# Half of w1 in row blocks of 128, 128, 96 and 96: a decode step with cached attention and a small dense layer

## The chip, the cores and the metric

The kernel runs on one core of one Trainium2 chip. The metric is the device time of one execution in microseconds (us); the median of several runs is compared. Differences of about 0.2% of this kernel's time can be told from no change.

## The reference

The kernel mixes two branches by a gate that is computed from the input:

```python
x = A_x                                            # [2, 1, 448]
g = sigmoid((x * gate_w).sum(-1, keepdims=True))
q = (x @ wq) as 16 heads of 256
p = softmax(q . k_cache * 256**-0.5)               # over 4096 cached keys
a = (p . v_cache, heads joined) @ wo               # [2, 1, 448]
b = relu(x @ w1) @ w2                              # w1 [448, 1792], w2 [1792, 448]
return g * a + (1 - g) * b
```

Everything is float32. The caches are [2, 16, 4096, 256] each; with the weights some 290 MB are read for one output of 2 x 448 numbers.

## The kernel before

The work of attention is cut into U = 32 units, one for each pair of batch and head. A unit's keys and values lie in DRAM as one row of 65,536 B for each of 128 partitions, 8.4 MB. On the chip there is a ring of three slots of that size (SLOTS, `slot`). SP issues all loads, in the order in which they are written in `sync` (L153 on): at first the query weights `wq` into slot 0 together with the input's columns `xg`, then kv 0 and 1 (L67 to L69, before the block); kv 2 when the query matmuls are done (L156); then, in a loop, the next unit into a slot as soon as DVE has freed it (L161, L162). Two loads stand in the queue at any time. The tail of the list is written out: the last kv unit in two halves (L167, L168), `w1` and `w2` into slot 0 (L170, L171) once unit 30 is freed from it, and `wo` in six pieces into slot 1 (L175), last the output (L178).

For a unit PE computes the scores from the keys (L131), DVE their maximum (L351), ACT the exponential and its sum (L318), and DVE eight products with the values (L356), the last of which signals `freed`.

The dense layer and the joining lie in `pe_tail`. `hidden` computes x @ w1 in the PSUM tile `pa`. The 1792 columns of w1 are four groups g of FG = 448; group g fills partitions 32g to 32g+31 of `pa`, each row holding x of one of the two batch entries, repeated. The 448 rows of w1, over which is contracted, are three blocks c of 128 (`x_of(c)`, L111) and a last one of 64. The blocks of 64 of two column groups are stacked on 128 partitions and contracted in one matmul of 64 output rows with `xl`, a tile that has x in one half and zeros in the other (L114). So `hidden` has 3 x 4 + 2 = 14 matmuls; each appears twice in the trace, as two passes for float32. It is called in three parts, between which PE does the small steps of the softmax tail: blocks 0 and 1 after the wait for `w1_in` (L231, L232); then, after the last unit is freed, two transposes (L234, L235) and block 2; then, after `wb_ok`, one small matmul and the last block. ACT applies the relu (L327), PE transposes (L250, L252), ACT copies (L329, L332), and PE accumulates the product with w2 in `acc` (L258). The wo product is accumulated in the same tile (L270) as its pieces land; DVE copies `acc` (L375), and PE folds it into `z` with the last pieces of wo (L278, L283), which DVE copies for the output (L377).

At the start ACT makes the broadcast copies of x: `xr` for the blocks of 128, `xn` for the gate, `xl` for the stacked blocks of 64 (L297 to L301); the last of them signals `x_ok`, for which PE's first matmul waits (L193).

Of the kernel before, what the change touches and what calls it, by code (L numbers as in the profile page):

```python
# [4 lines left out]
AF = mybir.ActivationFunctionType  # L5
# [4 lines left out]
P, HP = 128, 64  # L10
G = 4
R = P // G
# [3 lines left out]
DIRECT = (3, 2, 1)  # L16


def gated_mix_decode(nc, wq, kv, wm, wo, out):
    U, _, SW = kv.shape  # L20
    D = 448
    B = 2
    RB = R // B
# [4 lines left out]
    KC, KF = 4, 3  # L28
    H = U // B
    HH = H // G  # L30
    NW = wq.shape[1] - KC * (B + 1)
    FG = 448
    NF = 14
    W1 = 2 * (2 * KF * FG + FG)
    DG = D // G
    NO = HH * J
    SCALE = float(DH) ** -0.5
    pe, dve, act, pool, sp = nc.tensor, nc.vector, nc.scalar, nc.gpsimd, nc.sync
# [12 lines left out]
    slot = [ring[:, i * SW:(i + 1) * SW] for i in range(SLOTS)]  # L51

    def sb(name, *shape):
        t = nc.alloc_sbuf_tensor(name, list(shape), F32)
        assert nc.sbuf_base <= first
        return t.ap()
# [6 lines left out]
    last_v, w1_in, w2_in = ev(), ev(), ev()  # L63
# [11 lines left out]
    xr = sb("xr", P, KF, P // B, B)  # L75
    xl = sb("xl", P, 2, RB, B)
    xn = sb("xn", P, P // B, B)
    ge = sb("ge", P, 1)
    gp = sb("gp", P, 1)
    omg = sb("omg", P, 1)  # L80
# [7 lines left out]
    p = sb("p", P, SG)  # L88
# [10 lines left out]
    pa = ps("pa", P, CW)  # L99
# [5 lines left out]
    def x_of(c, n=R):  # L105
        return xr[:, c].rearrange("p r b -> p (r b)")[:, :n]

    def project(dst, w, at, at_last, n, lo, hi):
        for c in range(lo, min(hi, KF)):
            for g in range(G):  # L110
                m = pe.matmul(dst[g * R:(g + 1) * R, :n], x_of(c), w[:, at(c, g):at(c, g) + n], start=(c == 0), stop=False)  # L111
        if hi == KC:
            for i in range(2):
                m = pe.matmul(dst[i * HP:(i + 1) * HP, :n], xl.rearrange("p j r b -> p (j r b)"),  # L114
                              w[:, at_last(i):at_last(i) + n], start=False, stop=True)
        return m

    xg = slot[0][:, NW:wq.shape[1]].rearrange("p (c b) -> p c b", c=KC)

    ident_0, ident_ok, par_ok, fold_ok, xl_0 = (ev() for _ in range(5))  # L120
    x_ok, gate_mm, gate_ok, ge_ok, gp_ok, omg_ok = (ev() for _ in range(6))
# [23 lines left out]
    ml_tr, nb_ok, e_ok, el_ok, rl_ok, wb_ok, wp_mm, os_ok, po_mm, oc_ok = (ev() for _ in range(10))  # L145
    acc_mm, a_ok, z_mm, res_ok = ev(), ev(), ev(), ev()
    w1 = slot[0][:, :W1]
    w2 = slot[0][:, W1:W1 + NF * D]
    w_o = slot[1]

    with nc.Block(no_gpsimd_drain=True) as block:

        @block.sync  # L153
        def _(_e):
            sp.wait_ge(q_mm, 2)
            sp.dma_start(slot[0], kv[2]).then_inc(slot_in[0], 16)  # L156
            with nc.Fori(0, LOOP - 2, engines=(ET.SP,)) as r:
                u0 = sp.snap(r * SLOTS)
                for k in range(SLOTS):
                    s = (k + 1) % SLOTS  # L160
                    sp.wait_ge(freed, u0 + k + 1)  # L161
                    sp.dma_start(slot[s], kv[bass.ds(u0 + k + SLOTS, 1)].rearrange("o p n -> (o p) n")  # L162
                                 ).then_inc(slot_in[s], 16)
            sp.wait_ge(freed, U - 4)
            sp.dma_start(slot[1], kv[U - 2]).then_inc(slot_in[1], 16)
            sp.wait_ge(freed, U - 3)
            sp.dma_start(slot[2][:, :SW // 2], kv[U - 1][:, :SW // 2]).then_inc(slot_in[2], 16)  # L167
            sp.dma_start(slot[2][:, SW // 2:], kv[U - 1][:, SW // 2:]).then_inc(last_v, 16)  # L168
            sp.wait_ge(freed, U - 2)
            sp.dma_start(w1, wm[:, :W1]).then_inc(w1_in, 16)  # L170
            sp.dma_start(w2, wm[:, W1:]).then_inc(w2_in, 16)  # L171
            sp.wait_ge(freed, U - 1)
            k = 0
            for n, s in zip(ACC + DIRECT, wo_in):
                sp.dma_start(w_o[:, k * D:(k + n) * D], wo[:, k * D:(k + n) * D]).then_inc(s, 16)  # L175
                k += n
            sp.wait_ge(res_ok, 1)
            sp.dma_start(out, res[0:7 * 15 + 1:7, :]).then_inc(out_sem, 16)  # L178
# [13 lines left out]
        def pe_main():  # L192
# [7 lines left out]
            for i in range(2):  # L200
                if i:
                    pe.wait_ge(q_ok, i)
                project(pb, slot[0][:, i * NW // 2:(i + 1) * NW // 2], lambda c, g: g * W + c * CW,
                        lambda i: G * W + i * CW, CW, 0, KC).then_inc(q_mm, 1)
# [18 lines left out]
                pe.end_ifs()  # L223

        def pe_tail():
            half = W1 // 2
            def hidden(lo, hi):
                return project(pa, w1, lambda c, g: g // 2 * half + (g % 2 * KF + c) * FG,
                               lambda i: i * half + 2 * KF * FG, FG, lo, hi)

            pe.wait_ge(w1_in, 16)  # L231
            hidden(0, 2)  # L232
            pe.wait_ge(freed, U)
            pe.transpose(pc[:U, :P], nm, ident)  # L234
            pe.transpose(pc[:U, P:2 * P], ls, ident).then_inc(ml_tr, 1)  # L235
            hidden(2, KF)
            pe.wait_ge(wb_ok, 1)
            pe.matmul(pb[:, :U], wb.rearrange("u g r -> u (g r)"), ident[:U, :U], start=True,
                      stop=True).then_inc(wp_mm, 1)
            hidden(KF, KC).then_inc(hid_mm, 1)  # L240
            pe.wait_ge(fold_ok, 1)
            pe.wait_ge(os_ok, 1)
            n = HH * B * J
            for g in range(G):
                m = pe.matmul(pc[g * R:(g + 1) * R, :n], sel,
                              os.rearrange("p u j -> p (u j)")[:, g * n:(g + 1) * n], start=True, stop=True)
            m.then_inc(po_mm, 1)
            pe.wait_ge(hid_ok, 1)
            for t in range(KF):
                pe.transpose(pb[:, t * P:(t + 1) * P], hs[:, t * P:(t + 1) * P], ident)  # L250
            for j in range(2):
                m = pe.matmul(pb[j * HP:(j + 1) * HP, KF * P:], hs[:, KF * P:], ident, start=True, stop=True)  # L252
            m.then_inc(hid_tr, 1)
            pe.wait_ge(w2_in, 16)
            pe.wait_ge(hr_ok, 1)
            for k in range(NF):
                g = k % G
                pe.matmul(acc[g * R:(g + 1) * R, :D], hr[:, k, :], w2[:, k * D:(k + 1) * D], start=(k < G),  # L258
                          stop=False)

            def o_of(k):
                return oc[:, k // J, k % J].rearrange("p r b -> p (r b)")

            pe.wait_ge(oc_ok, 1)
            k, n = 0, sum(ACC)
            for i, a in enumerate(ACC):
                pe.wait_ge(wo_in[i], 16)
                for _ in range(a):
                    g = k % G
                    m = pe.matmul(acc[g * R:(g + 1) * R, :D], o_of(k), w_o[:, k * D:(k + 1) * D], start=False,  # L270
                                  stop=(k >= n - G))
                    k += 1
            m.then_inc(acc_mm, 1)
            for i, a in enumerate(DIRECT):
                if i == 0:
                    pe.wait_ge(a_ok, 1)
                    for g in range(G):
                        pe.matmul(z[g * R:(g + 1) * R, :DG], fold.rearrange("p r b -> p (r b)"),  # L278
                                  a_sb[:, g * DG:(g + 1) * DG], start=(i == 0), stop=False)
                pe.wait_ge(wo_in[len(ACC) + i], 16)  # L280
                for _ in range(a):
                    for g in range(G):
                        m = pe.matmul(z[g * R:(g + 1) * R, :DG], o_of(k),  # L283
                                      w_o[:, k * D + g * DG:k * D + (g + 1) * DG], start=False,
                                      stop=(k == NO - 1))
                    k += 1
            m.then_inc(z_mm, 1)
# [7 lines left out]
        def _(_e):  # L295
            act.wait_ge(slot_in[0], 16)
            act.activation(xr, xg[:, :KF, None, :B].to_broadcast([P, KF, P // B, B]), AF.Copy)  # L297
            act.activation(xn, xg[:, KF:, :B].to_broadcast([P, P // B, B]), AF.Copy)
            act.wait_ge(xl_0, 1)
            for j in range(2):  # L300
                a = act.activation(xl[j * HP:(j + 1) * HP, j], xg[j * HP:(j + 1) * HP, KF:, :B]  # L301
                                   .to_broadcast([HP, RB, B]), AF.Copy)
            a.then_inc(x_ok, 1)
            act.wait_ge(gate_mm, 1)
# [1 line left out]
            for i in range(2):  # L306
# [3 lines left out]
                a = act.activation(qt[:, i * U // 2:(i + 1) * U // 2, :].rearrange("p (s n) t -> p s t n", s=2),  # L310
                                   pc.rearrange("p (s t x) -> p s t x", s=2, t=T)[:, :, :, ::17], AF.Copy)
# [18 lines left out]
            for j in range(2):  # L330
                r = slice(j * HP, (j + 1) * HP)
                a = act.activation(hr[r, KF * G:, :],  # L332
                                   pb[r, KF * P + j * HP:KF * P + (j + 1) * HP].rearrange("p (k r) -> p k r", r=R),
                                   AF.Copy)
# [103 lines left out]
```

## Time and profile before

| | |
|---|---|
| median of 3 runs | 676.48 us (676.44 to 677.43) |
| the profiled execution | 676.38 us |
| its span, first to last instruction | 674.8 us |
| mean granted TensorE clock | 0.676 |
| read from DRAM | 289.54 MB, 429 GB/s over the span |
| busy: PE, DVE, ACT | 213.0, 339.8, 54.2 us |
| DMA packets | 6082 |

The engines' busy times say how much of the span each one works. The profile's slices divide the span into 40 equal parts and give for each a tenth of busy share by engine, the clock, and what the DMA engines moved. The row of a DMA queue gives packets, megabytes and the time that the packets took, as a share of sixteen DMA engines' span. The chain that ended last is followed back from the last instruction; a row of it says when a piece began, how long it lasted and whose work it was. A row of the timeline gives the start, the duration, the engine and line, the operation, and in brackets the idle time before it with what ended it. A row of the view of windows gives, for one stretch, the length, each engine's busy time, the granted clock, the DMA share and the rate.

### The profile page before, as it was taken

What the parts mean: (1) busy time and instruction counts of PE and PEld (TensorE: products, weight loads), DVE (VectorE), ACT (ScalarE), POOL (GpSimd) and SP (SyncE); (2) the same over time, 40 slices, a digit from 0 to 9 for tenths busy, and PEclk for the clock granted to TensorE, in tenths of its full rate; (3) what the DMA queues carried; (4) which work ended last, traced back from release to release, by engine and by line L of the source; (5) the groups of instructions that cost most, each with busy time, mean ns of one, the idle gap of its engine ahead of it and who ended that gap; (6) DMA issues with size and microseconds to landing.
All of it is one profiled execution on the core that took longest, in us unless ns stands there. A gap on an engine that the chain in (4) does not pass through costs nothing.

```text
span 674.8 us, 4173 instructions
## 1 busy us (share of the span) xinstructions
PE 213.0 (32%) x1279; PEld 52.0 (8%) x1279; DVE 339.8 (50%) x561; ACT 54.2 (8%) x144; POOL 1.1 (0%) x9
## 2 busy tenths in 40 slices
PE   0633221333332123333321233333222333332455
PEld 0210000000000000000000000000000000000011
DVE  0024566545455665544656654455566445456670
ACT  0110000000000000000000000000000000000110
POOL 0000000000000000000000000000000000000000
PEclk9976567767655676776656677665667767655879
DMA  9999999999999999999999999999999999999997
GB/s 381 427 435 436 435 435 435 435 435 435 435 435 435 435 435 435 435 435 435 431 435 435 435 435 435 435 435 435 435 435 435 435 435 435 435 435 406 420 437 304
DMA packets 6082, 289.59 MB, mean 429 GB/s; under 512 B 704, under 2 KB 832, under 8 KB 1216
## 3 DMA queue, kind: packets, MB, share of 16 engines
q1 hardware_dynamic: 6080, 289.55, 99.3%
q8 instruction: 2, 0.03, 0.0%
HBM read 289.54 MB, written 0.01 MB: 429 GB/s over the span
## 4 chain that ended last, share of the span: by engine, by line
DMA 70%; DVE 12%; PE 9%; issue 6%; DVEq 1%; ACT 1%; SPq 0%; ACTq 0%
DMA ring<-in_kv 65%; DVE ring L356 10%; PE sc L131 9%; DMA ring<-in_wo 4%; DVE nm L351 2%; DVEq L356 1%; ACT p L318 1%; PE z L283 0%; DVEq L348 0%; DVEq L353 0%; PE acc L270 0%; SPq L175 0%; SPq L162 0%; DVEq L351 0%; DVE a_sb L375 0%
## 5 line engine op out<-in xcount | busy, mean ns | idle before, releaser
L356 DVE SCALAR_TENSOR_TENSOR ring<-ring,p 128x1024 f32 x256 | 295.9, 1222 | 54.8 <-ACT p L318 54.8
L131 PE MATMUL sc<-ring,qc 128*32 128x512 f32 x1024 | 182.6, 878 | 417.8 <-DMA ring<-in_kv 417.8
L351 DVE TENSOR_REDUCE nm<-sc 128x1024 f32 x32 | 39.2, 1225 | 236.1 <-PE sc L131 236.1
L131 PEld LDWEIGHTS sc<-ring,qc 128*32 128x32 f32 x1024 | 41.2, 154 | 558.6 <-issue 558.6
L318 ACT ACTIVATE p<-sc,nm 128x1024 f32<-128x1024 f32 x32 | 35.7, 1114 | 257.8 <-DVE nm L351 257.8
L323 ACT ACTIVATE ov<-on 128x8 f32 x32 | 6.7, 208 | 309.0 <-DVE ring L356 309.0
L356 DVE DVE_READ_ACCUMULATOR ring<-ring,p 128x1 f32 x256 | 21.4, 83 | 0.0
L343 DVE TENSOR_SCALAR ge<-ge 128x1 f32<-128x1 f32 x1 | 0.2, 155 | 21.5 <-ACT ge L305 21.5
L196 PE MATMUL pa<-ring,xr 128*128 128x1 f32 x6 | 1.4, 356 | 21.4 <-ACT xl L301 21.4
L375 DVE COPY a_sb<-acc 128x448 f32<-128x448 f32 x1 | 0.6, 625 | 14.7 <-PE acc L270 14.7
L111 PE MATMUL pa<-ring,xr 128*32 128x448 f32 x24 | 4.2, 830 | 11.7 <-DMA ring<-in_wm 11.7
L270 PE MATMUL acc<-ring,oc 128*32 128x448 f32 x52 | 5.9, 544 | 4.7 <-DMA ring<-in_wo 4.7
L111 PE MATMUL pb<-ring,xr 128*32 128x512 f32 x48 | 7.1, 737 | 0.0
L318 ACT ACTIVATION_READ_ACCUMULATOR p<-sc,nm x32 | 6.2, 193 | 0.0
L320 ACT ACTIVATE qc<-qt x32 | 6.1, 192 | 0.0
L258 PE MATMUL acc<-ring,hr 128*32 128x448 f32 x28 | 3.2, 541 | 1.0 <-ACT hr L332 1.0
L196 PEld LDWEIGHTS pa<-ring,xr 128*128 128x128 f32 x6 | 1.4, 326 | 21.4 <-ACT xl L301 21.4
L270 PEld LDWEIGHTS acc<-ring,oc 128*32 128x32 f32 x52 | 1.7, 109 | 8.9 <-issue 5.9
L114 PE MATMUL pb<-ring,xl 128*64 128x512 f32 x8 | 2.2, 618 | 0.0
L297 ACT ACTIVATE xr<-ring 128x384 f32<-128x384 f32 x1 | 0.5, 522 | 18.3 <-DMA ring<-in_wq 18.3
L111 PEld LDWEIGHTS pb<-ring,xr 128*32 128x32 f32 x48 | 1.6, 132 | 3.9 <-issue 3.9
L308 ACT ACTIVATE q<-pb 128x512 f32<-128x512 f32 x2 | 1.2, 598 | 8.6 <-PE pb L114 8.6
(56 smaller groups left out, 23.7 us busy)
## 6 DMA issues: line engine op xcount, KB each, us to landing
ring<-in_kv SPq DMA_DIRECT2D x2, 4096.0 KB, 34.7
ring<-in_wq SPq DMA_DIRECT2D x1, 7174.0 KB, 19.5
ring<-in_wm SPq DMA_DIRECT2D x2, 3136.0 KB, 30.7
ring<-in_wo SPq DMA_DIRECT2D x1, 3136.0 KB, 24.4
ring<-in_wo SPq DMA_DIRECT2D x1, 1792.0 KB, 28.3
ring<-in_wo SPq DMA_DIRECT2D x1, 896.0 KB, 30.0
ring<-in_wo SPq DMA_DIRECT2D x1, 672.0 KB, 31.1
ring<-in_kv SPq DMA_DIRECT2D x31, 39.6
```

What stands on the lines that cost most here:

```text
L111: m = pe.matmul(dst[g * R:(g + 1) * R, :n], x_of(c), w[:, at(c, g):at(c, g) + n], start=(c == 0), stop=False)
L114: m = pe.matmul(dst[i * HP:(i + 1) * HP, :n], xl.rearrange("p j r b -> p (j r b)"), w[:, at_last(i):at_last(i) + n], start=False, stop=True)
L131: m = pe.matmul(sc[g * R:(g + 1) * R, c * CW:(c + 1) * CW], qc[:, s, t:t + 1].to_broadcast([P, R]), slot[s][:, lo:lo + CW], start=(t == 0) ...
L196: m = pe.matmul(pa[:, :1], x_of(c, P) if c < KF else xn[r].rearrange("p r b -> p (r b)"), xg[r, c, B:], start=(c == 0), stop=(c == KC - 1))
L258: pe.matmul(acc[g * R:(g + 1) * R, :D], hr[:, k, :], w2[:, k * D:(k + 1) * D], start=(k < G), stop=False)
L270: m = pe.matmul(acc[g * R:(g + 1) * R, :D], o_of(k), w_o[:, k * D:(k + 1) * D], start=False, stop=(k >= n - G))
L308: act.activation(q, pb, AF.Copy, scale=SCALE).then_inc(q_ok, 1)
L318: act.activation(p, sc, AF.Exp, bias=nm[:, bass.ds(u, 1)], accum_out=ls[:, bass.ds(u, 1)]).then_inc(raised, 1)
L320: act.activation(qf[:, bass.ds((u + 2) % SLOTS * T, T)], qt[:, bass.ds(u + 1, 1), :].rearrange("p o t -> p (o t)"), AF.Copy).then_inc(quer ...
L323: act.activation(ov[:, bass.ds(u, 1), :].rearrange("p o j -> p (o j)"), on, AF.Copy).then_inc(kept, 1)
L351: dve.tensor_reduce(nm[:, bass.ds(u, 1)], sc, axis=AX.X, op=ALU.max, negate=True).then_inc(maxed, 1)
L356: m = dve.scalar_tensor_tensor(v, v, 1.0, p, op0=ALU.mult, op1=ALU.mult, accum_out=on[:, j:j + 1])
```

## The change

The four column groups of w1 are split into two halves of two groups each. The first half (groups 0 and 1) is as before: three blocks of 128 rows and the stacked blocks of 64. In the second half (groups 2 and 3) the 448 rows are cut into blocks of 128, 128, 96 and 96. The blocks of 128 of both halves and the stacked blocks lie in `wm` and are loaded as `w1`, 4928 numbers to a row in place of 6272. The 96-row blocks lie in an array of their own, `we`, of shape [12, 9, 11200]: a row is 11,200 numbers, 44,800 B, of which the first 1792 are data; of nine rows in a group eight are data. One more DMA, between those of w1 and w2, loads the [12, 8, 1792] numbers onto 96 partitions of slot 0 (`w1e`). It adds to the same semaphore, and PE waits for both loads.

Rows of x: block 2 of the second half is rows 256 to 351, which `xr`'s block 2 has in its first 96 partitions; block 3 is rows 352 to 447, for which there is a new tile `xe`, a broadcast by ACT of a new column block of `xg`, which makes a row of `wq` 12 B longer. Blocks 2 and 3 of the second half are contracted with 96 rows. `hidden` has 15 matmuls: 8 for blocks 0 and 1, 4 for block 2, and 3 for block 3 (one stacked for the first half, two of 96 rows for the second). The host code that lays out the arrays changes accordingly.

```diff
-    W1 = 2 * (2 * KF * FG + FG)
+    PS = 96
+    W1 = 2 * KF * FG + FG + 4 * FG
+    WE = 4 * FG
...
+    xe = sb("xe", P, RB, B)
...
     w1 = slot[0][:, :W1]
-    w2 = slot[0][:, W1:W1 + NF * D]
+    w1e = slot[0][:PS, W1:W1 + WE]
+    w2 = slot[0][:, W1 + WE:W1 + WE + NF * D]
...
             sp.dma_start(w1, wm[:, :W1]).then_inc(w1_in, 16)
+            sp.dma_start(w1e, we[:, :8, :WE]).then_inc(w1_in, 16)
             sp.dma_start(w2, wm[:, W1:]).then_inc(w2_in, 16)
...
-            half = W1 // 2
+            half = 2 * KF * FG + FG
+
             def hidden(lo, hi):
-                return project(pa, w1, lambda c, g: g // 2 * half + (g % 2 * KF + c) * FG,
-                               lambda i: i * half + 2 * KF * FG, FG, lo, hi)
-
-            pe.wait_ge(w1_in, 16)
+                for c in range(lo, hi):
+                    for g in range(G):
+                        i, h = divmod(g, 2)
+                        if i == 0 and c == KF:
+                            if g == 0:
+                                pe.matmul(pa[:HP, :FG], xl.rearrange("p j r b -> p (j r b)"),
+                                          w1[:, 2 * KF * FG:half], start=False, stop=True)
+                            continue
+                        x, at = x_of(c) if c < KF else xe.rearrange("p r b -> p (r b)"), (h * KF + c) * FG
+                        if i:
+                            at = half + (h * 2 + c) * FG if c < 2 else (h * 2 + c - 2) * FG
+                        w = w1e if i and c >= 2 else w1
+                        m = pe.matmul(pa[g * R:(g + 1) * R, :FG], x[:PS] if w is w1e else x, w[:, at:at + FG],
+                                      start=(c == 0), stop=(c == KC - 1))
+                return m
+
+            pe.wait_ge(w1_in, 32)
...
-            act.activation(xn, xg[:, KF:, :B].to_broadcast([P, P // B, B]), AF.Copy)
+            act.activation(xn, xg[:, KF:KC, :B].to_broadcast([P, P // B, B]), AF.Copy)
+            act.activation(xe, xg[:, KC:, :B].to_broadcast([P, RB, B]), AF.Copy)
...
+    rest = w1[2 * P:, 1].reshape(2, PS, 2, FG).transpose(1, 2, 0, 3).reshape(PS // 8, 8, -1)
+    we = np.zeros((PS // 8, 9, 25 * FG), np.float32)
+    we[:, :8, :rest.shape[2]] = rest
```

More of the change, by code (lines that the diff above doesn't have):

```diff
@@ L16, with gated_mix_decode @@
 DIRECT = (3, 2, 1)
-def gated_mix_decode(nc, wq, kv, wm, wo, out):
+def gated_mix_decode(nc, wq, kv, wm, we, wo, out):
     U, _, SW = kv.shape
@@ L30, in gated_mix_decode @@
     HH = H // G
-    NW = wq.shape[1] - KC * (B + 1)
+    NW = wq.shape[1] - (KC + 1) * (B + 1)
     FG = 448
     NF = 14
-    W1 = 2 * (2 * KF * FG + FG)
+    PS = 96
+    W1 = 2 * KF * FG + FG + 4 * FG
+    WE = 4 * FG
     DG = D // G
@@ L116, in project @@
         return m
-    xg = slot[0][:, NW:wq.shape[1]].rearrange("p (c b) -> p c b", c=KC)
+    xg = slot[0][:, NW:wq.shape[1]].rearrange("p (c b) -> p c b", c=KC + 1)
     ident_0, ident_ok, par_ok, fold_ok, xl_0 = (ev() for _ in range(5))
@@ L297, in _ @@
             act.activation(xr, xg[:, :KF, None, :B].to_broadcast([P, KF, P // B, B]), AF.Copy)
-            act.activation(xn, xg[:, KF:, :B].to_broadcast([P, P // B, B]), AF.Copy)
+            act.activation(xn, xg[:, KF:KC, :B].to_broadcast([P, P // B, B]), AF.Copy)
+            act.activation(xe, xg[:, KC:, :B].to_broadcast([P, RB, B]), AF.Copy)
             act.wait_ge(xl_0, 1)
             for j in range(2):
-                a = act.activation(xl[j * HP:(j + 1) * HP, j], xg[j * HP:(j + 1) * HP, KF:, :B]
+                a = act.activation(xl[j * HP:(j + 1) * HP, j], xg[j * HP:(j + 1) * HP, KF:KC, :B]
                                    .to_broadcast([HP, RB, B]), AF.Copy)
@@ L404 @@
     full, last = blocks(np.concatenate([np.asarray(A_x).reshape(B, D).T, np.asarray(gate_w).reshape(D, 1)], 1))
-    xg = np.concatenate([full, np.concatenate([last, last])[:, None]], 1)
+    PS = 96
+    ext = np.zeros((P, 1, B + 1), np.float32)
+    ext[:PS, 0] = np.concatenate([full[PS:, KF - 1], last])
+    xg = np.concatenate([full, np.concatenate([last, last])[:, None], ext], 1)
     kt = np.asarray(A_k_cache)[:, heads].reshape(B, H, S, T, P).transpose(1, 0, 4, 3, 2).reshape(U, P, T * S)
@@ L416 @@
     wo = np.asarray(A_wo).reshape(HH, G, R, J, D).transpose(1, 2, 0, 3, 4).reshape(P, -1)
-    full, last = blocks(B_w1)
-    full = full.reshape(P, KF, 2, 2, FG).transpose(0, 2, 3, 1, 4).reshape(P, 2, -1)
-    last = last.reshape(HP, 2, 2, FG).transpose(2, 0, 1, 3).reshape(P, 2, FG)
-    w1 = np.concatenate([full, last], 2).reshape(P, -1)
+    w1 = np.asarray(B_w1).reshape(D, 2, 2, FG)
+    full, last = blocks(w1[:, 0])
+    full = full.reshape(P, KF, 2, FG).transpose(0, 2, 1, 3).reshape(P, -1)
+    last = last.reshape(HP, 2, FG).transpose(1, 0, 2).reshape(P, FG)
+    both = w1[:2 * P, 1].reshape(2, P, 2, FG).transpose(1, 2, 0, 3).reshape(P, -1)
+    rest = w1[2 * P:, 1].reshape(2, PS, 2, FG).transpose(1, 2, 0, 3).reshape(PS // 8, 8, -1)
+    we = np.zeros((PS // 8, 9, 25 * FG), np.float32)
+    we[:, :8, :rest.shape[2]] = rest
+    w1 = np.concatenate([full, last, both], 1)
     w2 = np.asarray(B_w2).reshape(G, FG, D)
@@ L424 @@
     w2 = np.concatenate([full, last], 1).reshape(P, -1)
-    arrays = {"wq": wq, "kv": kv, "wm": np.concatenate([w1, w2], 1), "wo": wo}
+    arrays = {"wq": wq, "kv": kv, "wm": np.concatenate([w1, w2], 1), "we": we, "wo": wo}
     arrays = {n: np.ascontiguousarray(a) for n, a in arrays.items()}
```

## The prediction

> **What bounds the kernel now.** I read the page's slices and queue first, then the chain that ended last, then the tail in time.
>
> ```profile
> DMA  9999999999999999999999999999999999999997
> GB/s 381 427 435 436 435 435 435 435 435 435 435 435 435 435 435 435 435 435 435 431 435 435 435 435 435 435 435 435 435 435 435 435 435 435 435 435 406 420 437 304
> q1 hardware_dynamic: 6080, 289.55, 99.3%
> DMA 70%; DVE 12%; PE 9%; issue 6%; DVEq 1%; ACT 1%; SPq 0%; ACTq 0%
> ```
>
> All sixteen DMA engines are busy from the first slice to the last, on one queue, which fills 99.3% of sixteen engines' span. The rate is flat at 435 GB/s: 435/16 = 27.2 GB/s for each engine. The bytes of each engine therefore set the end, whatever wait the chain names. The tail shows it closer, first the chain from the window behind 638 us:
>
> ```profile
> 638.55 0.43 SPq L175
> ...
> 639.02 29.95 DMA ring<-in_wo
> 668.98 0.04 issue
> 669.02 1.00 PE acc L270 x8
> 670.02 0.02 issue
> 670.05 0.64 DVE a_sb L375
> 670.68 0.04 issue
> 670.73 0.40 PE z L278 x8
> 671.12 1.53 PE z L283 x48
> ```
>
> The last 30 us are the wo loads, queued behind w1 and w2; some 3.7 us of PE and DVE work follow. If a landing moves, the end moves with it. Profiled and unprofiled time: the span is 674.8 us, the execution 676.38 us, so 1.6 us lie outside; the median of the three runs, 676.48 us, is 0.10 us above that execution.
>
> **The engines do not end together.** The DMA view of 670 to 672.4 us (slices of 0.06 us), and the one of 659 to 662 us:
>
> ```profile
> DMA  9988453301111020020201100000000000000000
> GB/s 448 358 329 299 150 209 119 120 0 60 60 60 60 0 90 30 30 90 0 90 30 60 60 0 30 30 30 30 30 30 0 0 0 0 0 0 0 0 0 0
> ...
> q1 hardware_dynamic: 103, 0.18, 19.0%
> ...
> q8 instruction: 1, 0.02, 2.0%
> ```
>
> Most engines are done at about 670.5 us; one or two (a tenth is 1.6 engines) go on to 671.8 us. An instruction fetch, the last row, accounts for most of that: one packet that took 2.0% of 16 x 3 us = 0.96 us of one engine. So a straggler, about 1.3 us behind the pack, sets the end. The few left do not run faster while the others are idle: in this window the queue moved 0.18 MB in 19.0% of 16 x 2.4 us = 7.3 us of engine time, 25 GB/s for a busy engine. An engine's 27.2 GB/s is a limit of its own way, not a share of a common pool.
>
> **The change part by part.**
>
> *Bytes.* w1 is 128 rows x 6272 numbers = 3136 KB. After, it is 128 x 4928 (2464 KB) and 96 x 1792 (672 KB): 3136 KB again. Nothing is saved. The wq load grows by 12 B a row, 1.5 KB in all: 4 ns at 435 GB/s.
>
> *The cut of the 96 rows.* In every load of before, 128 rows are 8 for each of 16 engines. The new load's source is 12 groups of 8 rows, its target 96 partitions, and no load of before shows how that is cut. Two bounds. Cut evenly, each engine gets 6 rows of 7168 B in place of 8 x 5376 B of the old w1: equal bytes. Cut by the groups, twelve engines get 8 rows each, 57,344 B, against the 43,008 B they lose from w1: 14,336 B more, at 27.2 GB/s 0.53 us; the other four carry 43,008 B less, 1.58 us. To this come packets. The DMA view of 668 to 674 us:
>
> ```profile
> DMA packets 361, 0.99 MB, mean 165 GB/s; under 512 B 50, under 2 KB 178, under 8 KB 361
> q1 hardware_dynamic: 361, 0.99, 40.9%
> ```
>
> 40.9% of 16 x 6 us is 39.3 us; 0.99 MB at 27.2 GB/s is 36.4 us; the rest, 2.9 us over 361 packets, is 8 ns each. Eight more on an engine: 0.06 us. Thus even cut +0.06 us, cut in twelve +0.59 us. I take twelve: it is the largest count up to sixteen that leaves each group of the source whole.
>
> [...]
>
> *Whether twelve engines get twelve ways.* The 27.2 GB/s may belong to the engine or to the way from it into the eight partitions that it writes; in all loads of before the two coincide. In the new load the blocks of eight rows are cut out of 96, so two engines may meet on one way. Bounds: no meeting, nothing; two meeting throughout, each of an engine's 8 packets takes twice as long: 8 x 7168 B / 27.2 GB/s = 2.11 us more. I take the upper end, because the slices show a limit with no spare width: 435 or 436 in nearly every kv slice of the page, none above, and no higher rate for an engine that is left alone. A second stream on a way like that cannot be absorbed.
>
> [...]
>
> *Which engine ends last, then.* If the straggler is one of those that meet, the end moves by 0.59 + 2.11 = 2.70 us. If it isn't, the pack overtakes it: 670.5 + 2.70 = 673.2 us against 671.8 us, 1.4 us later. The more of the twelve meet, the likelier the straggler is among them, so I lean to the larger and take +2.5 us.
>
> *Rows 44,800 B apart.* The w1 and w2 rows of before are 50,176 B apart (25,088 B each out of two); their stage, from the view of windows:
>
> ```profile
> 640.00:656.00 16.00, 7.17 (x47) 2.08 (x47) 11.88 (x26) 2.52 (x9) 0.00 (x0) 0.68 1.03 442
> ```
>
> 442 GB/s at a share of 1.03 (edges of packets) are 429 at a full one, within 2% of kv's contiguous rows at 435, and the change makes the distance smaller. I take nothing; if the reads lost as much as the lowest late slice of the page (406 against 435), 672 KB would cost 0.1 us.
>
> *The issue.* One more DMA on SP, between those of L170 and L171:
>
> ```profile
> 619.99 0.33 SPq L170 DMA_DIRECT2D ring<-in_wm  x1
> 620.36 0.43 SPq L171 DMA_DIRECT2D ring<-in_wm  x1
> 638.18 2.70 SPq L175 DMA_DIRECT2D ring<-in_wo  x6
> ```
>
> 0.43 us more puts L171 at 620.8 us; SP then waits for the DVE until 638.18 us, and the queue works on kv until then. Free by 17 us.
>
> *The wait of PE.* w1_in now needs both loads. Behind it on PE's queue stand the first hidden matmuls, then the two transposes that open the softmax tail, then all that DVE and ACT do with them.
>
> ```profile
> 647.26 3.21 PE L111 MATMUL pa<-ring,xr 128*32 128x448 f32 x16 [11.73 <-DMA ring<-in_wm]
> 650.40 0.40 PE L234 MATMUL pc<-ident,nm 128*32 128x128 f32 x1
> ...
> 652.62 0.97 PE L114 MATMUL pa<-ring,xl 128*64 128x448 f32 x4
> ...
> 656.25 3.20 PE L258 MATMUL acc<-ring,hr 128*32 128x448 f32 x28 [1.01 <-ACT hr L332]
> 662.72 1.71 PE L270 MATMUL acc<-ring,oc 128*32 128x448 f32 x16 [3.27 <-DMA ring<-in_wo]
> ```
>
> w1 complete 0.6 to 2.7 us later starts L111 at 647.9 to 650.0 us. Transposes and tail follow 0.6 to 2.7 us later, and L258 ends at 660.1 to 662.2 us in place of 659.45 us. The cover is the 3.27 us that PE waits for wo before L270; moreover wo moves along with w1. The matmuls go from 14 to 15 (two thin ones and a wide one in place of two wide ones): at most half of the 0.97 us row, 0.5 us. Worst case 662.7 us: just at the old L270, and wo is then later too. So nothing of it reaches the end; with the cover gone it would cost the excess, 0.5 us or less.
>
> *The start.* ACT makes one more broadcast, xe. Nearest row: xn with four times the columns; beside it the SP rows at the start.
>
> ```profile
> 20.71 0.29 ACT L298 ACTIVATE xn<-ring 128x128 f32<-128x128 f32 x1
> 33.76 0.33 SPq L156 DMA_DIRECT2D ring<-in_kv  x1
> 57.81 40.62 SPq L162 DMA_DIRECT2D ring<-in_kv  x3
> ```
>
> At most 0.29 us on the way to the query matmuls, and so on SP's L156 at 33.76 us. The two kv loads issued before it, 8.4 MB or 19.3 us each at 435 GB/s, keep the queue full from 20 us to 58 us: 24 us of cover. Nothing.
>
> **The sum.** 676.38 + 2.5 = 678.9 us for the profiled execution; with the 0.10 us of the median 679.0 us.
>
> **The rivals.**
>
> *Twelve engines, no meeting* (not slower by a measurable amount). The surplus of 0.59 us is all: 677.1 us. For it: nothing in the trace of before shows two engines slowing one another. Against it: the flat ceiling per engine. It decides if rows in an engine's block of eight need no shared way.
>
> *The straggler is among the four spared engines.* Without meeting, its end moves from 671.8 to 670.2 us and the pack's from 670.5 to 671.1 us: the span ends 0.7 us earlier, 675.8 us. For it: four of sixteen engines are spared, and the fetch stands on one engine. It needs no meeting and that engine: a quarter of the case above.
>
> *The load is cut evenly, so that the change of engines doesn't occur.* +0.06 us, 676.5 us. For it: 96 also divides by 16; against it, the groups of the source would be split.
>
> *More meetings.* The spared engines and those that finish first are already in w2, whose rows of 25,088 B take 0.92 us each, and may meet the rest. One such row doubled: 2.70 + 0.92 = 3.6 us, 680.1 us.
>
> **How the numbers follow.** A measurement of this kernel can tell about 0.2%, 1.35 us, from no change. Meeting in twelve engines has 0.55, with +1.4 to +2.7 us; more meetings 0.04; no meeting 0.29; the spared straggler 0.06; the even cut 0.04; a gain from a cause that I don't see 0.02. The first two are slower by over 0.2%, except some 0.03 at the lower edge: 0.56. Within 0.2% are the three middle cases and that edge, less 0.02 for a spared straggler whose gain is larger than worked out: 0.40. That 0.02 and the unseen gain make 0.04 for faster. The likeliest case alone spans 677.9 to 679.2 us. The range reaches down to the even cut and a no-meeting run with scatter, 676.4 us, and up to the further meetings, 680.1 us.
>
> **What would show it.** Bandwidth in the slice in which w1's second part moves (about 645 to 650 us) should fall clearly under 435 GB/s; PE's wait at L111's successor should end 2 to 3 us later than 647.26 us; the wait before L270 should end about 2.5 us later than 662.72 us; kv's slices should stay as they are. If the first landing moves by 0.6 us only, no engines meet. If the landings of w1 and wo do not move at all, the cut was even. The forecast is wrong if the end moves without w1's landing, or if the fetch falls on another engine or another moment, which would shift the end by up to the straggler's 1.3 us for a reason that the sum doesn't hold.

## The result, and the profile after

The changed kernel takes 679.58 us, the median of 11 runs (677.26 to 681.64); the kernel before takes 676.48 us (675.95 to 677.53, 11 runs). The ratio is 1.0041 with a 95% interval of 1.0028 to 1.0054: slower by 3.1 us. The forecast was 679.0 us, slower.

The execution that was profiled is the fastest of those eleven: 677.26 us, with a span of 675.6 us, 0.8 us more than before. Traces of this kernel show the mechanism, therefore, but only a part of the 3.1 us; this is taken up below. From its page, the rate by slices and the packets; the last row is the packets before:

```profile
GB/s 381 431 431 436 435 435 435 435 435 435 435 435 435 435 435 435 435 435 435 435 435 435 435 435 435 435 435 435 435 435 435 435 435 435 435 435 433 422 376 331
DMA packets 6190, 289.59 MB, mean 429 GB/s; under 512 B 716, under 2 KB 844, under 8 KB 1324
...
DMA packets 6082, 289.59 MB, mean 429 GB/s; under 512 B 704, under 2 KB 832, under 8 KB 1216
```

The kv slices are as they were; the loss lies in the 39th slice, 376 GB/s where 437 stood. The number of packets under 512 B went from 704 to 716. Before, these are sixteen for each of 43 loads and stores, the completions, one for each engine, and the 16 rows of the output. So the new load has twelve completions: it runs on twelve engines. Under 8 KB there are 108 more: the 96 rows and these twelve.

The DMA view of 643.5 to 648 us, the time in which the 96 rows move, first of the changed kernel, then of the kernel before:

```profile
DMA packets 142, 1.26 MB, mean 281 GB/s; under 512 B 25, under 2 KB 25, under 8 KB 118
q1 hardware_dynamic: 142, 1.26, 111.4%
```

```profile
DMA packets 96, 2.01 MB, mean 446 GB/s; under 512 B 16, under 2 KB 16, under 8 KB 16
q1 hardware_dynamic: 96, 2.01, 103.6%
```

A share above 100% comes from packets that reach over the edges of the window; the rate divided by the share is what counts: 281/1.114 = 252 GB/s against 446/1.036 = 430 GB/s. All engines are occupied and move 0.59 of what they did. In the trace's packet records 16 of the 96 packets of 7168 B take 272 ns and 56 take 500 ns or more; the mean is 467 ns. Rows of w2 beside them, 931 ns otherwise, take up to 1816 ns. Added up, the packets of the new load are 18.8 us longer than at 272 ns each, those of w1 0.8 us and those of w2 12.9 us: 32.5 us of engine time, 2.0 us for each of sixteen engines.

The traces don't number the engines. But a packet begins within a few ns of the end of one before it (4 ns before that end in the median), so that the packets can be threaded into sixteen chains; what is said below of single engines rests on this. Twelve chains have eight rows of the new load each, and four have none. The 2.0 us are not only a mean: each of the twelve loses about that, 1.3 to 2.0 us on its own eight rows and the rest on w2's, and each of the four spared engines loses 2.0 us as well, on rows of w1 and w2.

The tail, by the chain from 638 us on and by the view of 670 to 672.8 us (slices of 0.07 us):

```profile
639.15 30.60 DMA ring<-in_wo
...
669.80 1.00 PE acc L289 x8
```

```profile
DMA  9999996976998898969796959688787653000000
```

Before, fourteen engines ended by 670.5 us and two stragglers, each delayed by an instruction fetch (0.96 us each, at 62.96 and at 659.82 us), at 671.4 and 671.9 us. Now most engines are busy to about 672.3 us and the last ends at 672.7 us; the engines that the fetches delayed are among the four spared ones and no longer come last. The pack moved by about 2 us and has overtaken the stragglers; the end moved by 0.8 us (669.80 in place of 669.02 us for the last PE step on `acc`).

### The profile page after: what moved, and what is told of

It reads as the page before. It is cut to its first block, busy times and chain, and to the rows that moved or that the text cites. A ratio compares the mean times of both kernels' runs of the same rounds, so it can differ in the third digit from the quotient of the medians.

```text
span 675.6 us, 4179 instructions
## 1 busy us (share of the span) xinstructions
PE 213.6 (32%) x1281; PEld 52.4 (8%) x1281; DVE 339.8 (50%) x561; ACT 54.3 (8%) x145; POOL 1.1 (0%) x9
## 4 chain that ended last, share of the span: by engine, by line
DMA 69%; DVE 12%; PE 10%; issue 6%; DVEq 1%; ACT 1%; SPq 0%; ACTq 0%
DMA ring<-in_kv 65%; DVE ring L376 10%; PE sc L134 9%; DMA ring<-in_wo 5%; DVE nm L371 2%; DVEq L376 1%; ACT p L338 1%; PE z L302 0%; DVEq L368 0%; DVEq L373 0%; PE acc L289 0%; SPq L180 0%; SPq L166 0%; DVEq L371 0%; DVE a_sb L395 0%
## 5 line engine op out<-in xcount | busy, mean ns | idle before, releaser
L246 PE MATMUL pa<-ring,xr 128*32 128x448 f32 (+1 forms) x24 | 4.1, 803 | 15.4 <-DMA ring<-in_we 15.4
L289 PE MATMUL acc<-ring,oc 128*32 128x448 f32 x52 | 5.9, 544 | 1.6 <-DMA ring<-in_wo 1.6
L277 PE MATMUL acc<-ring,hr 128*32 128x448 f32 x28 | 4.9, 809 | 1.0 <-ACT hr L352 1.0
L392 DVE COPY oc<-pc 128x256 f32<-128x256 f32 x4 | 1.4, 418 | 1.5 <-PE pc L264 1.5
L289 PEld LDWEIGHTS acc<-ring,oc 128*32 128x32 f32 x52 | 1.7, 109 | 5.8 <-DMA ring<-in_wo 3.0
```

The costliest lines, as they stand in the source:

```text
L246: m = pe.matmul(pa[g * R:(g + 1) * R, :FG], x[:PS] if w is w1e else x, w[:, at:at + FG], start=(c == 0), stop=(c == KC - 1))
```

## The experiments

Theory W: the load runs on twelve engines in blocks of eight partitions, and engines that write different blocks can share one way of about 27 GB/s (435/16) into the target. Which blocks share is read from e5, e6, e9 and e10, by whole ranges: with an extra load on partitions 0 to 63, 32 to 95, 0 to 31 and 64 to 95 their windows show 223, 429, 429 and 221 GB/s. By these, blocks on 0 to 31 and on 32 to 63 have some eight ways together (223/27.2), and blocks on 32 to 95 some sixteen (429/27.2). The rivals: S, the 14,336 B more of the twelve engines are the cost; D, the distance of the source rows or the 96-row matmuls are.

Times are medians; each is compared with runs of the kernel before that were taken beside it.

| run | what | against before, us | ratio, 95% interval |
|---|---|---|---|
| e1_pad128 | the 96 rows loaded as 128 | 677.05 - 676.42 = +0.63 | 1.0010 (1.0002 to 1.0019) |
| e2_even96 | 96 rows, source not grouped | 678.43 - 676.42 = +2.01 | 1.0034 (1.0022 to 1.0047) |
| e3_packed12 | source rows 7168 B apart | 678.70 - 676.42 = +2.28 | 1.0040 (1.0024 to 1.0055) |
| e4_split | 64 rows on 32 to 95, then 32 rows | 677.56 - 676.42 = +1.14 | 1.0018 (1.0009 to 1.0026) |
| e5_x64_lo | extra load on partitions 0 to 63 | 681.77 - 676.35 = +5.42 | 1.0080 (1.0067 to 1.0093) |
| e6_x64_mid | the same on partitions 32 to 95 | 678.58 - 676.35 = +2.23 | 1.0031 (1.0020 to 1.0043) |
| e7_after | the changed kernel again | 679.18 - 676.35 = +2.83 | 1.0048 (1.0030 to 1.0066) |
| e9_x32_lo | extra load, 8 engines, 0 to 31 | 677.65 - 676.19 = +1.46 | 1.0023 (1.0014 to 1.0032) |
| e10_x32_hi | the same on partitions 64 to 95 | 679.23 - 676.19 = +3.04 | 1.0052 (1.0034 to 1.0070) |

**e1_pad128: the same rows over all 128 partitions.** 32 unused rows are added, so that the load has the cut of every other load.

```diff
-    w1e = slot[0][:PS, W1:W1 + WE]
+    w1e = slot[0][:, W1:W1 + WE]
...
-            sp.dma_start(w1e, we[:, :8, :WE]).then_inc(w1_in, 16)
+            sp.dma_start(w1e, we[:, :WE]).then_inc(w1_in, 16)
...
-    we = np.zeros((PS // 8, 9, 25 * FG), np.float32)
-    we[:, :8, :rest.shape[2]] = rest
+    we = np.zeros((128, 25 * FG), np.float32)
+    we[:PS, :rest.shape[1]] = rest
```

> The 96 rows are loaded as 128, of which the last 32 are not used; row distance and matmuls as in the changed kernel. [...] Theory D (the distance of the source rows, or the 96-row matmuls, cost the 3.1 us): still about +3.1 us.

+0.63 us. The same window of its trace:

```profile
DMA packets 203, 1.93 MB, mean 429 GB/s; under 512 B 32, under 2 KB 32, under 8 KB 160
q1 hardware_dynamic: 203, 1.93, 101.1%
```

429/1.011 = 424 GB/s, and all 128 packets take 272 ns. The source distance and the 96-row matmuls are those of the changed kernel, so D falls. Every engine carries 14,336 B more here, as the twelve do there, and that costs 0.6 us, near the 0.53 us estimated from 27.2 GB/s: S cannot be the 3.1 us.

**e2_even96: the source not grouped.** The ninth rows go, the array is [96, 11200].

```diff
-            sp.dma_start(w1e, we[:, :8, :WE]).then_inc(w1_in, 16)
+            sp.dma_start(w1e, we[:, :WE]).then_inc(w1_in, 16)
```

> The source is 96 plain rows, 44,800 B apart, without the ninth row of each group, so that sixteen engines can carry 6 rows each. [...] S: no engine has more bytes, +0.06 us, packets at 272 ns. D: as the changed kernel, +3.1 us.

+2.01 us, as W would have it (rows 0 to 31 and 32 to 63 are still loaded together) and against S: the load has sixteen completions (720 packets under 512 B), so no engine has bytes more, yet most of the loss is there. The same window:

```profile
DMA packets 159, 1.48 MB, mean 329 GB/s; under 512 B 31, under 2 KB 31, under 8 KB 127
q1 hardware_dynamic: 159, 1.48, 108.8%
```

329/1.088 = 302 GB/s. The number of engines is thus not the point; that the 96 rows are cut otherwise than 128 are is.

**e3_packed12: source rows close together.** Only the length of a source row changes.

```diff
-    we = np.zeros((PS // 8, 9, 25 * FG), np.float32)
+    we = np.zeros((PS // 8, 9, 4 * FG), np.float32)
```

> Groups of eight and a ninth row as in the changed kernel, but rows 7168 B apart in place of 44,800 B. W and S: no difference to the changed kernel, about +3 us and packets near 540 ns. D: the loss goes, +0.6 us.

+2.28 us, with an interval that overlaps the changed kernel's. Its packets average 455 ns (467 ns there). The 44,800 B between rows cost nothing that can be seen.

**e4_split: the rows laid so that most of them do not meet.** The array is that of e2.

```diff
-            sp.dma_start(w1e, we[:, :8, :WE]).then_inc(w1_in, 16)
+            sp.dma_start(w1e[32:], we[32:, :WE]).then_inc(w1_in, 16)
+            sp.dma_start(w1e[:32], we[:32, :WE]).then_inc(w1_in, 16)
...
-            pe.wait_ge(w1_in, 32)
+            pe.wait_ge(w1_in, 48)
```

> The 96 rows go in two loads: 64 rows on partitions 32 to 95, then 32 rows on partitions 0 to 31. W: the first load has sixteen engines on sixteen ways (nobody meets), the second sixteen engines on eight ways, two rows each: +0.53 us and 0.1 us of packets, so +0.6 us, up to +1.2 us if the meeting spreads to w2. S: 6 rows for every engine, +0.1 us. D: about +3.1 us.

+1.14 us, at the upper end of what W expected, and under e2, which moves the same rows in one load (the two intervals overlap a little). Of its 96 packets 82 take 272 ns, where e2 has 23. By W the 32 rows on partitions 0 to 31 should have taken twice that; most did not, and the excess stands on w2's rows behind them: 9.1 us of engine time, 0.6 us an engine. Its size fits W's 0.53 us, its place doesn't: the delay shows on the packets behind those that should meet. In the changed kernel, too, the first row of each engine takes 272 ns. Why it comes late, no run shows.

**e5_x64_lo and e6_x64_mid: the same load in two places.** To the kernel before is added one load that nothing uses. The two kernels differ in one number, the first target partition.

```diff
+            sp.dma_start(slot[0][0:64, W1 + NF * D:W1 + NF * D + 8 * FG], wm[:64, :8 * FG]).then_inc(w2_in, 16)
             sp.dma_start(w2, wm[:, W1:]).then_inc(w2_in, 16)
...
-            pe.wait_ge(w2_in, 16)
+            pe.wait_ge(w2_in, 32)
```

In e6 the slice is `32:96`.

> The kernel before with one more load, which nothing uses, between w1 and w2: 64 rows of 14,336 B onto partitions 0 to 63, four rows for each of sixteen engines. [...] Rival: the engines' own rate is the limit, +2.1 us, packets at 535 ns.

> The same extra load of the same source rows, but onto partitions 32 to 95. W: sixteen engines reach sixteen ways, +2.1 us, packets at 535 ns. Rival (a load of 64 partitions is slow wherever it lies): +4.2 us.

+5.42 and +2.23 us. The windows of 645.5 to 650 us, e5 first:

```profile
DMA packets 80, 1.09 MB, mean 242 GB/s; under 512 B 16, under 2 KB 16, under 8 KB 16
q1 hardware_dynamic: 80, 1.09, 108.4%
```

```profile
DMA packets 142, 2.10 MB, mean 466 GB/s; under 512 B 31, under 2 KB 31, under 8 KB 31
q1 hardware_dynamic: 142, 2.10, 108.7%
```

223 GB/s against 429 GB/s, at the same share. On partitions 32 to 95 all 64 packets take 535 ns; on 0 to 63 they average 1007 ns. Engines, bytes and source are equal, so the limit is that of the way into the target. By W every engine meets another in e5, and four rows of 14,336 B at half of 27.2 GB/s take 4 x 527 ns x 2 = 4.2 us (an estimate). The extra 1.2 us over that have two parts in e5's trace. Most engines lose 4.5 us from the end of kv to the end of wo's first piece, w2's rows included. The straggler, which comes to the load over 1.1 us after the others, loses 5.8 us and ends wo 2.5 us behind most of them. Exactly one other engine loses more on its rows, 6.0 us in all, with two rows of w2 (2.08 and 1.90 us) that move while the straggler's last rows do: a pair, as W has it.

**e9_x32_lo and e10_x32_hi: eight engines, two targets.** The source is grouped so that eight engines carry four rows each.

```diff
+            sp.dma_start(slot[0][0:32, W1 + NF * D:W1 + NF * D + 8 * FG],
+                         wm.rearrange("(a b) n -> a b n", b=8)[:8, :4, :8 * FG]).then_inc(w2_in, 16)
             sp.dma_start(w2, wm[:, W1:]).then_inc(w2_in, 16)
...
-            pe.wait_ge(w2_in, 16)
+            pe.wait_ge(w2_in, 32)
```

In e10 the slice is `64:96`.

> The kernel before with one more load, which nothing uses, between w1 and w2: 32 rows of 14,336 B in 8 groups of 4 onto partitions 0 to 31, so that eight engines get four rows each, 2.1 us of work, and the other eight none. W (shared ways): each of the eight writes a way of its own, packets at 535 ns. The end: the eight reach it 2.1 us later, and the stragglers, 1.3 us behind the pack in the kernel before, are among the eight that got nothing, as in the traces of the changed kernel: +0.8 us with little scatter. If the stragglers are on other engines in some of the runs: times between +0.8 and +2.1 us in groups, which would explain the scatter of the changed kernel. A rival for which the target does not matter gives the same time here as in the run beside it.

> The same extra load from the same source rows on the same eight engines, but onto partitions 64 to 95. W: these are the ways of the other eight engines, which are in w2 then; both sides are held, packets of the extra load near 1070 ns and 64 of w2's packets lengthened, the eight end 4.2 us later, the others 2.1 us: +2.8 to +4.2 us. Rival (only the bytes of an engine count): as the run beside it, +0.8 to +2.1 us.

+1.46 and +3.04 us. The windows of 645.5 to 648 us, e9 first:

```profile
DMA packets 87, 1.24 MB, mean 495 GB/s; under 512 B 24, under 2 KB 24, under 8 KB 24
q1 hardware_dynamic: 87, 1.24, 115.5%
```

```profile
DMA packets 41, 0.64 MB, mean 255 GB/s; under 512 B 7, under 2 KB 7, under 8 KB 7
q1 hardware_dynamic: 41, 0.64, 115.6%
```

429 GB/s against 221 GB/s. In e9 the 32 packets take 535 ns and no row of w2 is lengthened; in e10 they average 964 ns and w2's rows lose 21.0 us of engine time. The other eight engines, which are in w2 by then, lose 2.1 us each on its rows: by W these are what the eight meet, for among themselves they do not (in e6 all packets, those on 64 to 95 among them, took 535 ns). This is the second half of the mechanism: the extra load holds up the load behind it.

**e7_after, then e8_look_a to e8_look_c: the scatter.** The changed kernel again, six executions and then three single ones.

> The changed kernel once more, for its scatter and a second trace. W: +2 to +4 us; its packets of 7168 B near 540 ns again; the time differs from run to run by how far the meeting engines stand apart and whether the straggling engine is among them.

+2.83 us; packets of 7168 B average 457 ns. The six runs fall in groups: 677.83 and 678.27, then 679.18 and 679.19, then 681.23 and 681.49 us, as the eleven before did (three up to 678.5, six from 679.23 to 679.67, two at 681.6). The kernel before and e1 have no such groups (675.8 to 677.8 and 676.3 to 678.2 us).

> One more look at the changed kernel, to catch a trace of a slower run than the two traces so far (677.3 and 678.3 us). If it falls near 679.6 or 681.6 us: by the theory of the straggler, the 7168 B packets end as early as in the two traces and one engine of the pairs that meet ends the wo loads 2 us or more behind the pack; by the theory of the meeting's length, the 7168 B packets themselves and the doubled w2 packets end 2 us later.

> As the look before it: straggler late behind an unchanged pack, or a longer meeting.

> As the look before it: straggler late behind an unchanged pack, or a longer meeting.

Inconclusive: 678.35, 677.56 and 677.80 us, all of the lowest group. In the five traces of the changed kernel the last PE step on `acc` begins 0.7 to 1.1 us later than in the trace of before. The six traces of grouped sources (the changed kernel five times, and e3) are alike: the 96 packets end 3.9 to 4.4 us after the first began, and the later half of wo's last 128 packets ends within 0.4 to 0.7 us. In all of them the engine that the first instruction fetch delayed is one of the four that got no rows. No trace of a run at 679.6 or 681.6 us exists.

## Why the prediction was right, point by point

**Bytes and the limit of each engine: right.** The kv slices stay at 435 GB/s, and the loss is where the new load runs.

**Twelve engines: right**, by the twelve completion packets and the twelve chains with eight rows each. The surplus was worth 0.59 us; e1, with the same surplus on all sixteen engines, took +0.63 us.

**Two engines on one way: right**, and shown by e5 against e6 and by e9 against e10, where the target alone changes and the rate halves (429 GB/s on partitions 32 to 95, 223 GB/s on 0 to 63; 429 GB/s on 0 to 31, 221 GB/s on 64 to 95), and by the pair of engines in e5. The runs show this for whole ranges; which single partitions share a way was not shown.

**Its size: near for an engine that meets, too narrow in scope.** The prediction doubled all eight packets of the engines that meet, 2.11 us each, and with the surplus put these engines 2.70 us later. In the trace the first packet of each of the twelve is not lengthened and the mean is 467 ns in place of 527, but rows of w2 are lengthened too, about 2.0 us an engine in all. From the end of kv to the end of wo's first piece the twelve take 24.8 us in place of 22.3: 2.5 us more. In this execution kv ended some 0.5 us earlier than in the one before the change, so the pack ended about 2 us later. The prediction left open how many meet; W gives 8 of the 12, those with rows 0 to 63, but all twelve and the four spared ones were held up. The spared ones lost 2.0 us, mostly on w2, and came out 0.4 us later where the prediction had them 1.58 us earlier. Lengthened rows of w2 were the forecast's rival of 0.04. That the four engines with rows 64 to 95 met the spared ones, as in e10, would fit; this is argued.

**Which engine ends last: the other way than it leaned, and the median not shown.** The forecast leaned to a straggler that is among the engines that meet, +2.5 us. In the traces the first fetch fell on an engine without rows in every kernel that left some without, eight traces out of eight (the changed kernel, e3, e9, e10). In the changed kernel's traces the pack overtakes the straggler, the branch that was priced at 1.4 us, and the end moves by 0.7 to 1.1 us. The median of +3.1 us is made by executions of which there is no trace. A straggler that meets could end some 2 us behind the pack, as it does in e5 (2.5 us), and that would fit the group 2 us up; but no trace has one in the changed kernel, the group 4 us up isn't worked out by it, and e9, where nobody meets but eight engines get more work, is spread too (676.80 to 679.51 us). The cause of the groups stays open. So the direction was right and the pack's delay near, but that the median came within 0.6 us of the forecast is in part luck: the step from the pack's delay to the end is unconfirmed.

**PE's wait and its cover: the cover held, but barely.** The timeline of PE:

```profile
648.87 3.11 PE L246 MATMUL pa<-ring,xr 128*32 128x448 f32 x16 [15.45 <-DMA ring<-in_we]
...
658.42 4.90 PE L277 MATMUL acc<-ring,hr 128*32 128x448 f32 x28 [1.02 <-ACT hr L352]
663.51 3.20 PE L289 MATMUL acc<-ring,oc 128*32 128x448 f32 x28 [0.20 <-DMA ring<-in_wo]
```

The first hidden matmul starts 1.61 us later than before, not 2 to 3 us, and the wait for wo ends 0.79 us later (663.51 in place of 662.72 us), not 2.5: both less than the signs that were named. A straggler had set the second one before: the last row of wo's first piece ended at 662.2 us then and at 663.0 us now. The w2 matmuls (L277, before L258) end at 663.3 us; 662.7 us was called the worst case. They took 4.90 us in place of 3.20, as the clock was low; from the view of windows:

```profile
658.00:660.00 2.00, 1.58 (x12) 0.70 (x16) 0.00 (x0) 0.26 (x2) 0.00 (x0) 0.64 1.11 477
660.00:662.00 2.00, 2.00 (x16) 0.57 (x11) 0.00 (x0) 0.00 (x0) 0.00 (x0) 0.50 0.90 385
```

The granted clock is 0.64 and 0.50 there, 1.00 in the same step before (656 to 660 us). Of the 3.27 us of cover 0.20 us are left. In e2 it was gone, and PE came to L289 without a wait; the next two groups of wo still made it wait 0.94 and 0.62 us, so the end did not move by it.

**Row distance: right** as far as can be seen, by e3. **The start: right.** SP's own waits show it, first after, then before, 0.3 us more and no change in kv's slices:

```profile
SPq L160 <- PE pb L117: 32.0, 1, 32.0
SPq L156 <- PE pb L114: 31.7, 1, 31.7
```

**The issue: hidden, but dearer than worked out.** The grouped source takes SP 1.03 us to issue, not 0.43:

```profile
618.78 1.03 SPq L175 DMA_DIRECT2D ring<-in_we  x1
```

## What to carry to other kernels

In a kernel that is bound by DMA, count for each load not only the bytes of an engine but where the engines write: here a load on partitions 0 to 63 ran at 223 GB/s and the same load on 32 to 95 at 429 GB/s, and one on 64 to 95 cost the load behind it 21.0 us of engine time, while the DMA share stood above 100% in each window. Divide the rate in a window by the DMA share: about 430 GB/s was a clean load here, about 220 GB/s the loads of e5 and e10, whose engines meet by W. If rows must be fewer, fill up to 128 partitions (0.6 us here for a third more bytes, against 2 to 3 us) or lay 64 of them on partitions 32 to 95 (1.1 us here, with the other 32 in a load of their own).

## What the runs showed of the hardware that was not expected

- 64 partitions are not slow as such: on 32 to 95 a load ran at the full 429 GB/s (e6), on 0 to 63 at 223 GB/s (e5).
- In the changed kernel's trace 56 of the 96 packets of 7168 B took 500 ns and more in place of 272, but the first ones of the load did not: 16 took 272 ns, the first of each of the twelve engines among them, and the delay ran on into w2's rows behind them (12.9 us of engine time).
- The w2 matmuls of the changed kernel took 4.90 us for the same 28 in the profiled execution, at a granted clock of 0.64 and 0.50 (658 to 662 us), and 3.20 us in e8_look_c, at 1.00, with nothing of the program changed between them.
